# Reading the moving columns of single-pass matmuls as two interleaved halves

## The chip, the cores and the metric

The kernel runs on one core of one Trainium2 chip. The metric is the device time of one execution in microseconds, median of several runs. Three runs of the kernel before took 2629.4, 2629.59 and 2632.5 us; the median is 2629.59 us.

## The reference

Two layers follow each other. The first mixes along the sequence in the frequency domain: a real FFT over 3008 positions of each of 8 sequences of 256 features, a complex product with a 256x256 weight plus bias, a soft threshold of 0.01 on the real and the imaginary part, and the inverse FFT. The second is a feed-forward layer on the 24064 resulting tokens: 256 features to 2048, then `h*cos(h)`, then back to 256. Everything is float32.

```
X = np.fft.rfft(x, axis=1)                       # x: 8 x 3008 x 256
Yr = Xr @ w_r - Xi @ w_i + b_r                   # soft threshold on Yr, Yi follows
Yi = Xr @ w_i + Xi @ w_r + b_i
y = np.fft.irfft(Y, n=3008, axis=1)
h = y.reshape(24064, 256) @ moe_w_in             # to 2048
out = (h * np.cos(h)) @ moe_w_out                # back to 256
```

## The kernel before

3008 is 47 times 64, so the transform is done as a DFT of length 47, one of length 64, the mixing, an inverse DFT of length 64 and an inverse DFT of length 47. Each batch (one sequence) passes four stages.

- **Stage A** (`stage_a`, first DFT-47): 32 units of 512 columns. The input is split into a high and a low part; one matmul with the constant `fas` (line 364) gives both products on two sets of partitions, and ACT and DVE add them on the way out (lines 366 and 367) into `ao`, which goes to DRAM scratch. Batches 0 and 1 have forms of their own (`stage_a0`, `stage_a1`).
- **Stage B** (`stage_b`): 12 units. `fwd` is the DFT-64 (line 396). `wmix` mixes features with three sums of two weights, 18 matmuls of 256 columns (lines 420 to 422), then bias and threshold. `idft` is the inverse DFT-64, three matmuls of 512 columns (line 460; in unit 0 six of 256), copied out by ACT (line 463). Batch 0 has `stage_b0`.
- **Stage C** (`stage_c`, inverse DFT-47): line 715, results split into `xTh` and `xTl`, the tokens of the feed-forward layer.
- **Feed-forward** (`moe_step`, `second`): for each batch six tiles of tokens, five of 512 and one of 448, and for each tile 16 chunks of 128 of the 2048 features. A step of one tile and chunk has six matmuls into `ph` (lines 772 to 774) and, three steps later, six into `po` (lines 742, 743, 748). Between them ACT and DVE form `h*cos(h)` and split it into `gh` and `gl` (lines 779 to 785).

Precision comes from splitting: a number is written as a high and a low part of type float32r, and a product is three float32r matmuls (high by high, low by high, high by low). Four places use whole float32 operands instead: lines 396 and 715, and the transforms of batches 0 and 1. The profile names both types f32 in a matmul's row; a float32 matmul stands in it as two records, a float32r matmul as one.

The order is the program's own (`tc.manual_schedule`): each feed-forward step calls `pull`, which takes pieces of the next batches' stages A, B and C by a budget of costs (`share`, the numbers that the stages yield). So stage work of later batches stands between the feed-forward matmuls of this one. PSUM has three banks for `ph`, three for all stage work (`fps`), and two for `po`.

Every moving operand of a matmul is read in before with its columns one after another. The feed-forward output has one column per token, and the host puts tokens in order at the end.

Of the kernel before, what the change touches and what calls it, by code (L numbers as in the profile page):

```python
# [17 lines left out]
ALU = mybir.AluOpType  # L18

NB, N, D, FF = 8, 3008, 256, 2048  # L20
# [7 lines left out]
NTT = 6  # L28
# [29 lines left out]
def _index():  # L58
    n1, n2 = np.arange(64), np.arange(48)
    return (47 * n1[:, None] + 64 * n2[None, :]) % N  # L60


def _constants():
# [50 lines left out]
def tile_body(ctx: ExitStack, tc, x, x2, w_r, w_i, b_r, b_i, w_in, w_out,  # L114
              c_fa, c_fas, c_fb, c_inv, c_sig, c_last, c_inf, out):
    nc = tc.nc
# [12 lines left out]
    fas = cp.tile([112, 128], F32R, name="fas")  # L129
    ident = cp.tile([128, 128], F32, name="ident")  # L130
    inv = cp.tile([128, 2, 2, 128], F32R, name="inv")
# [8 lines left out]
    inf, ws = {}, []  # L140
    wf = cp.tile([128, 3, 2, 2, 256], F32R, name="wf")
    win = cp.tile([128, 2, 2, FF], F32R, name="win")
    wo = [cp.tile([128, 2, NFC, 256], F32R, name="wout")]

    mm = nc.tensor.matmul

    def rest_pool(lo, x, hi):
        return nc.gpsimd.tensor_tensor(out=lo, in0=x, in1=hi.bitcast(F32), op=ALU.subtract)  # L148

# [11 lines left out]
        nc.vector.scalar_tensor_tensor(out=wi, in0=wi, scalar=-1.0, in1=wr, op0=ALU.mult, op1=ALU.subtract)  # L161

    def split_fourier_w(j):
        hi, lo = (wf[:, j, h].rearrange("p c e -> p (c e)") for h in range(2))
        nc.scalar.copy(hi, ws[j])
        rest_pool(lo, ws[j], hi)

    def load_f64(src, queue):
        if len(raws) < EARLY_W + TAIL_W:
# [63 lines left out]
    raws, mark = [], {}  # L233
# [101 lines left out]
    def stage_a(b):  # L335

        scr1[b] = dr.tile([24, 2, 64, 256], F32, tag="scr1", name=f"scr1_{b}")
        dst = scr1[b].rearrange("k r n d -> (k r) (n d)")
        ld = {}

        def load(i):
            if i < 32:
                g, c = i % 2, i // 2
                ld[i] = stage_in("xt")[:112]
                nc.sync.dma_start(ld[i], x2[b - 2, g, :, 512 * c:512 * (c + 1)])

        def prep(i):
            if i < 32:
                xt = ld[i]
                ld[i] = wk.tile([128, 512], F32R, tag="xh", name="xh", bufs=XH_BUFS)[:112]  # L350
                with tc.issue_after(mark["gh"].ins) if b == 2 else ExitStack():
                    nc.scalar.copy(ld[i], xt)  # L352
                (rest if i % A_DVE == 0 else rest_pool)(ld[i][64:], xt[64:], ld[i][64:])

        load(0)
        yield 0.0
        prep(0)
        yield 1.0
        for i in range(32):
            load(i + 1)  # L360
            prep(i + 1)
            g, c = i % 2, i // 2
            p = fps("pa")
            mm(p, fas, ld.pop(i), start=True, stop=True)  # L364
            ao = stage_out("ao")[:48]
            nc.scalar.copy(ao, p[:48])  # L366
            nc.vector.tensor_tensor(out=ao, in0=p[64:112], in1=ao, op=ALU.add)  # L367
            nc.sync.dma_start(dst[:, 8192 * g + 512 * c:8192 * g + 512 * (c + 1)], ao)
            yield 0.23

    def stage_b(b):
        scr2[b] = dr.tile([32, 2, 2, 24, 256], F32, tag="scr2", name=f"scr2_{b}")
        dst = scr2[b].rearrange("j g r k d -> (j g r) (k d)")
        at, fb, X, Z, V = {}, {}, {}, {}, {}
# [40 lines left out]
        def wmix(m):  # L415
            xh, xl = X.pop(m)

            def product(p, j, comp, first, stop):
                for c in range(2):
                    mm(p, xh[:, comp, c], wf[:, j, 0, c], start=first and c == 0, stop=False, skip_group_check=True)  # L420
                    mm(p, xh[:, comp, c], wf[:, j, 1, c], start=False, stop=False, skip_group_check=True)  # L421
                    mm(p, xl[:, comp, c], wf[:, j, 0, c], start=False, stop=stop and c == 1, skip_group_check=True)  # L422

            p1 = fps("p1")[:, :256]
            product(p1, 0, 2, True, True)
            k1 = [wk.tile([128, 256], F32, tag=f"k1{r}", name=f"k1{r}", bufs=2) for r in range(2)]
            nc.vector.tensor_tensor(out=k1[1], in0=p1, in1=bias[:, 1], op=ALU.add)
            nc.vector.tensor_tensor(out=k1[0], in0=p1, in1=bias[:, 0], op=ALU.add)
            nc.scalar.activation(k1[1], k1[1], AF.Copy, scale=sig[:, m:m + 1])
            yield 0.73  # L430
            p2 = fps("p2")
            product(p2[:, :256], 1, 1, True, False)
            yield 0.73
            product(p2[:, 256:], 2, 0, False, True)
            z = wk.tile([128, 2, 256], F32, tag="z", name="z", bufs=2)
            for k in range(2):
                ks = slice(64 * k, 64 * k + 64)
                nc.vector.tensor_tensor(out=z[:64, k], in0=p2[ks, :256], in1=k1[0][ks], op=ALU.add)
            for k in range(2):
                ks = slice(64 * k, 64 * k + 64)  # L440
                nc.vector.scalar_tensor_tensor(out=z[64:, k], in0=p2[ks, 256:], scalar=sig[ks, m:m + 1],
                                               in1=k1[1][ks], op0=ALU.mult, op1=ALU.add)
            z = z.rearrange("p k e -> p (k e)")
            cl = wk.tile([128, 512], F32, tag="cl", name="cl", bufs=1)
            nc.vector.tensor_scalar(out=cl, in0=z, scalar1=-LAM, scalar2=LAM, op0=ALU.max, op1=ALU.min)  # L445
            nc.gpsimd.tensor_tensor(out=z, in0=z, in1=cl, op=ALU.subtract)  # L446
            yh = wk.tile([128, 512], F32R, tag="yh", name="yh", bufs=2)
            yl = wk.tile([128, 512], F32R, tag="yl", name="yl", bufs=2)
            nc.scalar.copy(yh, z)
            rest_pool(yl, z, yh)  # L450
            V[m] = (yh, yl)
            yield 0.73

        def idft(m):
            p = fps("pi")
            parts = ((0, 256, 0), (256, 512, 1)) if m == 0 else ((0, 512, 1),)
            y = V.pop(m)
            for n, (h, y) in enumerate(((0, y[0]), (1, y[0]), (0, y[1]))):
                for lo, hi, v in parts:
                    mm(p[:, lo:hi], inv[:, h, v], y[:, lo:hi], start=n == 0 and lo == 0, stop=n == 2 and hi == 512,  # L460
                       skip_group_check=True)
            bo = stage_out("bo")
            nc.scalar.copy(bo, p)
            nc.sync.dma_start(dst[:, 512 * m:512 * m + 512], bo)
            yield 0.68

# [266 lines left out]
    def second(b, t, f, gh, gl):  # L733
        n = 512 if t < NTT - 1 else 448
        first, last_f = next((lo, hi - 1) for v, lo, hi in phases(b) if v == t and lo <= f < hi)
        if f == first:
            outs[0] = [ps.tile([128, 512], F32, tag=f"o{e}", name=f"po{e}", bufs=1) for e in range(2)]
        po = outs[0]
        end = (b, t, f) == (NB - 1, NTT - 1, NFC - 1)
        for e in range(2):  # L740
            es = slice(128 * e, 128 * e + 128)
            mm(po[e][:, :n], wo[0][:, 0, f, es], gh[:, :n], start=f == first, stop=False)  # L742
            mm(po[e][:, :n], wo[0][:, 1, f, es], gh[:, :n], start=False, stop=False)  # L743
            if end:
                mm(po[e][:, :n], wo[0][:, 0, f, es], gl[:, :n], start=False, stop=True)
        for e in range(0 if end else 2):
            es = slice(128 * e, 128 * e + 128)
            mm(po[e][:, :n], wo[0][:, 0, f, es], gl[:, :n], start=False, stop=f == last_f)  # L748
        if f != last_f:
            return  # L750
        for e in range(2):
            if last_f < NFC - 1:
                part[t, e] = wk.tile([128, 512], F32, tag=("yh", "yl", "z")[t], name="part", bufs=2)
                nc.scalar.copy(part[t, e], po[e])  # L754
                continue
            if e == 0:
                outs[1] = pool["mo"].tile([128, 2, 512], F32, tag="ob", name="ob", bufs=1)
            ob = outs[1][:, e]
            if first:
                nc.vector.tensor_tensor(out=ob, in0=po[e], in1=part.pop((t, e)), op=ALU.add)  # L760
            else:
                (nc.vector.tensor_copy if end and e else nc.scalar.copy)(ob[:, :n], po[e][:, :n])
            nc.sync.dma_start(out[b, e, :, 512 * t:512 * t + n], ob[:, :n])

    def moe_step(b, t, f, pull):
        th, tl = xT[b, t]
        n = 512 if t < NTT - 1 else 448
        ph = ps.tile([128, 512], F32, tag="h", name="ph", bufs=3)
        h = ph[:, :n]
        fs = slice(128 * f, 128 * f + 128)  # L770
        for c in range(2):
            mm(h, win[:, 0, c, fs], th[:, c, :n], start=c == 0, stop=False)  # L772
            mm(h, win[:, 0, c, fs], tl[:, c, :n], start=False, stop=False)  # L773
            mark["ph"] = mm(h, win[:, 1, c, fs], th[:, c, :n], start=False, stop=c == 1)  # L774
        u = pool["mo"].tile([128, 512], F32, tag="u", name="u", bufs=4)
        k = u.bitcast(I32)
        gh = pool["mo"].tile([128, 512], F32R, tag="gh", name="gh", bufs=SKEW + 1)
# [143 lines left out]
```

## Time and profile before

| | |
|---|---|
| runs | 2629.4, 2629.59, 2632.5 us |
| the profiled execution | 2629.45 us |
| its span, first to last instruction | 2627.7 us |
| busy | PE 2618.9, PEld 2241.8, DVE 1917.8, ACT 1877.2, POOL 1085.3 us |
| granted TensorE clock | 1.00 over the span |
| instructions on PE | 13180 matmuls, 13180 weight loads |

The profiled execution is 0.14 us under the median of the runs. PE is the array's matmuls, PEld its weight loads. The duration of one matmul in a row is from its start to its last result and holds a fixed time in the pipeline that overlaps the next matmul; what one costs the engine is the distance from its start to the next one's start. That distance is called the pitch below.

### The profile page before, as it was taken

The page shows a single profiled execution, that of the slowest core. Times are in us where ns is not written, and L with a number is a line of the kernel's source. Part 1 is how long each engine was busy: PE and PEld are TensorE (multiplying, and loading weights), DVE is VectorE, ACT ScalarE, POOL GpSimd, SP SyncE. Part 2 cuts the span into 40 slices and gives each one's busy share as a digit, 9 for nine tenths or more (in the row PEclk, how much of TensorE's full clock was granted, in tenths as well). Part 3 has the DMA queues.
Part 4 walks back from the last instruction along what each step waited for, and adds up shares of the span by engine and source line. Part 5 has one row for each costly group of instructions (what it writes and reads, how often), then busy time and mean ns, then how long its engine had stood idle before and what let it go on. Part 6 is the DMA issues. An engine that isn't in the chain of part 4 may idle for free.

```text
span 2627.7 us, 38433 instructions
## 1 busy us (share of the span) xinstructions
PE 2618.9 (100%) x13180; PEld 2241.8 (85%) x13180; DVE 1917.8 (73%) x3237; ACT 1877.2 (71%) x3557; POOL 1085.3 (41%) x916
## 2 busy tenths in 40 slices
PE   9999999999999999999999999999999999999999
PEld 8788888888888888888888888888888888888888
DVE  6888876877667776777767777677776666766665
ACT  5787766777677776777767777677776666666666
POOL 5774543544334443344423444244442333322222
PEclk9999999999999999999999999999999999999999
DMA  7533312322123222233212232123221111010000
GB/s 208 177 97 98 105 61 77 94 87 90 55 60 93 86 85 59 60 93 98 75 56 62 91 96 75 55 62 103 89 71 53 47 53 43 25 54 22 9 17 16
DMA packets 126373, 194.26 MB, mean 74 GB/s; under 512 B 14131, under 2 KB 63619, under 8 KB 126177
## 3 DMA queue, kind: packets, MB, share of 16 engines
q1 hardware_dynamic: 120160, 171.94, 21.5%
q0 software_dynamic: 6016, 19.86, 2.4%
q8 instruction: 104, 1.70, 0.3%
q14 instruction: 93, 0.75, 0.1%
HBM read 119.92 MB, written 71.83 MB: 73 GB/s over the span
## 4 chain that ended last, share of the span: by engine, by line
PE 99%; DMA 0%; DVE 0%; SPq 0%; issue 0%; ACT 0%; ACTq 0%
PE ph L772 13%; PE po L742 13%; PE po L743 13%; PE ph L773 13%; PE po L748 13%; PE ph L774 13%; PE pc L715 4%; PE pb L396 3%; PE p L422 2%; PE p L421 2%; PE p L420 2%; PE pi L460 2%; PE pa L364 2%; PE p L520 1%; PE pa L323 1%; PE pa L297 0%
## 5 line engine op out<-in xcount | busy, mean ns | idle before, releaser
L148 POOL TENSOR_TENSOR gl<-u,gh 128x512 fp32r<-128x512 f32 (+1 forms) x396 | 507.8, 1283 | 958.0 <-ACT gh L784 754.9
L783 DVE TENSOR_TENSOR u<-ph,u 128x512 f32<-128x512 f32 (+1 forms) x768 | 520.5, 678 | 275.6 <-ACT u L782 258.5
L780 DVE SCALAR_TENSOR_TENSOR u<-ph,u 128x512 f32<-128x512 f32 (+1 forms) x768 | 518.9, 676 | 252.0 <-ACT u L779 242.4
L779 ACT ACTIVATE u<-ph 128x512 int32<-128x512 f32 (+1 forms) x768 | 450.1, 587 | 253.0 <-PE ph L774 241.2
L782 ACT ACTIVATE u<-u 128x512 f32<-128x512 f32 (+1 forms) x768 | 479.5, 625 | 202.1 <-DVE u L780 199.1
L772 PE MATMUL ph<-xTh,win 128*128 128x512 f32 (+1 forms) x1536 | 611.5, 398 | 1.4 <-DVE u L783 1.1
L742 PE MATMUL po<-gh,wout 128*128 128x512 f32 (+1 forms) x1536 | 598.7, 390 | 0.0
L774 PE MATMUL ph<-xTh,win 128*128 128x512 f32 (+1 forms) x1536 | 595.1, 387 | 0.0
L773 PE MATMUL ph<-xTl,win 128*128 128x512 f32 (+1 forms) x1536 | 595.1, 387 | 0.0
L743 PE MATMUL po<-gh,wout 128*128 128x512 f32 (+1 forms) x1536 | 594.8, 387 | 0.0
L784 ACT CAST gh<-u 128x512 fp32r<-128x512 f32 (+1 forms) x768 | 467.2, 609 | 137.1 <-DVE u L783 134.9
L748 PE MATMUL po<-gl,wout 128*128 128x512 f32 (+1 forms) x1534 | 477.0, 388 | 0.0
L774 PEld LDWEIGHTS ph<-xTh,win 128*128 128x128 f32 x1536 | 288.8, 188 | 54.4
L742 PEld LDWEIGHTS po<-gh,wout 128*128 128x128 f32 x1536 | 289.0, 188 | 51.7 <-ACT part L754 0.3
L743 PEld LDWEIGHTS po<-gh,wout 128*128 128x128 f32 x1536 | 289.0, 188 | 51.6
L772 PEld LDWEIGHTS ph<-xTh,win 128*128 128x128 f32 x1536 | 289.1, 188 | 49.6 <-DVE u L783 2.0
L748 PEld LDWEIGHTS po<-gl,wout 128*128 128x128 f32 x1534 | 285.6, 188 | 51.9
L773 PEld LDWEIGHTS ph<-xTl,win 128*128 128x128 f32 x1536 | 289.5, 188 | 46.0
L151 DVE TENSOR_TENSOR gl<-u,gh 128x512 fp32r<-128x512 f32 (+1 forms) x372 | 274.2, 737 | 49.8 <-ACT gh L784 42.2
L148 POOL TENSOR_TENSOR xh<-xt,xh 48x512 fp32r<-48x512 f32 x144 | 188.5, 1310 | 205.9 <-ACT xh L352 179.4
L446 POOL TENSOR_TENSOR z<-z,cl 128x512 f32<-128x512 f32 x84 | 110.0, 1309 | 208.4 <-DVE cl L445 197.6
L367 DVE TENSOR_TENSOR ao<-pa,ao 48x512 f32<-48x512 f32 x192 | 133.0, 693 | 22.2 <-ACT ao L366 17.1
(122 smaller groups left out, 3108.1 us busy)
## 6 DMA issues: line engine op xcount, KB each, us to landing
xt<-in_dram SPq DMA_DIRECT2D x192, 224.0 KB, 2.7
scr<-bo SPq DMA_DIRECT2D x95, 256.0 KB, 2.0
bt<-scr SPq DMA_DIRECT2D x96, 240.0 KB, 3.2
at<-scr SPq DMA_DIRECT2D x84, 256.0 KB, 2.7
out_dram<-ob SPq DMA_DIRECT2D x80, 256.0 KB, 2.2
scr<-ao SPq DMA_DIRECT2D x192, 96.0 KB, 1.9
fb<-in_dram POOLq DMA_DIRECT2D x46, 256.0 KB, 3.3
raw<-in_dram POOLq DMA_DIRECT2D x14, 512.0 KB, 4.3
```

The lines of the kernel that those rows point to most:

```text
L148: return nc.gpsimd.tensor_tensor(out=lo, in0=x, in1=hi.bitcast(F32), op=ALU.subtract)
L742: mm(po[e][:, :n], wo[0][:, 0, f, es], gh[:, :n], start=f == first, stop=False)
L743: mm(po[e][:, :n], wo[0][:, 1, f, es], gh[:, :n], start=False, stop=False)
L748: mm(po[e][:, :n], wo[0][:, 0, f, es], gl[:, :n], start=False, stop=f == last_f)
L772: mm(h, win[:, 0, c, fs], th[:, c, :n], start=c == 0, stop=False)
L773: mm(h, win[:, 0, c, fs], tl[:, c, :n], start=False, stop=False)
L774: mark["ph"] = mm(h, win[:, 1, c, fs], th[:, c, :n], start=False, stop=c == 1)
L779: nc.scalar.activation(k[:, :n], h, AF.Identity, bias=0.25, scale=1.0 / TWO_PI)
L780: nc.vector.scalar_tensor_tensor(out=u[:, :n], in0=h, scalar=1.0 / TWO_PI, in1=k[:, :n], op0=ALU.mult, op1=ALU.subtract)
L782: nc.scalar.activation(u[:, :n], u[:, :n], AF.Sin, bias=HALF_PI, scale=TWO_PI)
L783: nc.vector.tensor_tensor(out=u[:, :n], in0=h, in1=u[:, :n], op=ALU.mult)
L784: mark["gh"] = nc.scalar.copy(gh[:, :n], u[:, :n])
```

## The change

Three views are added: `woven` reads a row of n columns in the order 0, n/2, 1, n/2+1, and so on; `unwoven` and `halves` are used by evictions to bring such a row back in order. `woven` is put on the moving operand of the float32r matmuls of the feed-forward layer (both products), of the mixing, of the inverse DFT-64 in units 1 to 11, and of stage A. The columns come out of the array in the woven order:

- In the feed-forward layer nothing undoes it: `ph` is woven once, `po` twice, all vector work between is column by column, and the host's index takes the double permutation (`_order`).
- In the mixing the weight is the moving operand. Its split form `wf` is stored in the opposite order once, so that the woven read gives the natural one.
- In the inverse DFT-64 and in stage A the evictions read PSUM with a step of two columns and write two contiguous halves.

```
+    def woven(v):
+        return v.rearrange("p (b a) -> p a b", b=2)
+    def unwoven(v):
+        return v.rearrange("p (a b) -> p b a", b=2)
+    def halves(v):
+        return v.rearrange("p (b a) -> p b a", b=2)
     def split_fourier_w(j):
-        hi, lo = (wf[:, j, h].rearrange("p c e -> p (c e)") for h in range(2))
-        nc.scalar.copy(hi, ws[j])
-        rest_pool(lo, ws[j], hi)
+        for c in range(2):
+            hi, lo = (woven(wf[:, j, h, c]) for h in range(2))
+            w = ws[j][:, 256 * c:256 * c + 256].rearrange("p (a b) -> p a b", b=2)
+            nc.scalar.copy(hi, w)
+            rest_pool(lo, w, hi)
...
-            mm(p, fas, ld.pop(i), start=True, stop=True)
+            mm(p, fas, woven(ld.pop(i)), start=True, stop=True)
             ao = stage_out("ao")[:48]
-            nc.scalar.copy(ao, p[:48])
-            nc.vector.tensor_tensor(out=ao, in0=p[64:112], in1=ao, op=ALU.add)
+            nc.scalar.copy(halves(ao), unwoven(p[:48]))
+            nc.vector.tensor_tensor(out=halves(ao), in0=unwoven(p[64:112]), in1=halves(ao), op=ALU.add)
...
-                    mm(p, xh[:, comp, c], wf[:, j, 0, c], start=first and c == 0, stop=False, skip_group_check=True)
+                    wh, wl = (woven(wf[:, j, h, c]) for h in range(2))
+                    mm(p, xh[:, comp, c], wh, start=first and c == 0, stop=False, skip_group_check=True)
...
-                    mm(p[:, lo:hi], inv[:, h, v], y[:, lo:hi], start=n == 0 and lo == 0, stop=n == 2 and hi == 512,
+                    mm(p[:, lo:hi], inv[:, h, v], woven(y) if m else y[:, lo:hi], start=n == 0 and lo == 0,
...
+            if m:
+                nc.scalar.copy(halves(bo), unwoven(p))
+            else:
+                nc.scalar.copy(bo, p)
...
-            mm(po[e][:, :n], wo[0][:, 0, f, es], gh[:, :n], start=f == first, stop=False)
+            mm(po[e][:, :n], wo[0][:, 0, f, es], woven(gh[:, :n]), start=f == first, stop=False)
...
-            mm(h, win[:, 0, c, fs], th[:, c, :n], start=c == 0, stop=False)
+            mm(h, win[:, 0, c, fs], woven(th[:, c, :n]), start=c == 0, stop=False)
```

The lines of the other matmuls of these products change in the same way. No instruction changes its place on any engine. The only rows that differ are the six that split the mixing weights `wr`, `wi` and `wc` into `wf` in the prologue. On ACT these stood before as

```order
L515 COPY Xf<-pb 128x512
L165 CAST wf<-wr 128x512
L326 COPY ao<-pa 96x512
L515 COPY Xf<-pb 128x512
L165 CAST wf<-wi 128x512
L326 COPY ao<-pa 96x512
L165 CAST wf<-wc 128x512
L201 ACTIVATE wm<-raw 128x512
```

and on ACT they stand now, with the line numbers of the changed kernel, as

```order
L539 COPY Xf<-pb 128x512
L185 CAST wf<-wr 128x128x2 x2
L346 COPY ao<-pa 96x512
L539 COPY Xf<-pb 128x512
L185 CAST wf<-wi 128x128x2 x2
L346 COPY ao<-pa 96x512
L185 CAST wf<-wc 128x128x2 x2
L221 ACTIVATE wm<-raw 128x512
```

Each of the three became two of half the size at the same place; the three subtractions on POOL that follow them did too.

## Rows read from the trace of the kernel before

**Rows 1.** The page, part 1: busy us (share of the span) xinstructions.

```profile
span 2627.7 us, 38433 instructions
...
PE 2618.9 (100%) x13180; PEld 2241.8 (85%) x13180; DVE 1917.8 (73%) x3237; ACT 1877.2 (71%) x3557; POOL 1085.3 (41%) x916
```

**Rows 2.** The page, part 4: the chain that ended last, by engine.

```profile
PE 99%; DMA 0%; DVE 0%; SPq 0%; issue 0%; ACT 0%; ACTq 0%
```

**Rows 3.** Timeline of PE: start us, us, engine line op out<-in xcount; feed-forward of 512.

```profile
2442.25 0.39 PE L772 MATMUL ph<-xTh,win 128*128 128x512 f32 x1
...
2450.41 0.39 PE L772 MATMUL ph<-xTh,win 128*128 128x512 f32 x1
```

**Rows 4.** Timeline of PE, feed-forward of 448 columns, up to the end.

```profile
2612.35 0.36 PE L772 MATMUL ph<-xTh,win 128*128 128x448 f32 x1
...
2617.21 0.36 PE L772 MATMUL ph<-xTh,win 128*128 128x448 f32 x1
...
2622.89 0.57 PE L745 MATMUL po<-gl,wout 128*128 128x448 f32 x2
```

**Rows 5.** Timeline of PE, mixing products of 256 columns.

```profile
1222.14 0.28 PE L420 MATMUL p<-wf,Xh 128*128 128x256 f32 x1
...
1222.85 0.40 PE L772 MATMUL ph<-xTh,win 128*128 128x512 f32 x1
1223.08 0.28 PE L420 MATMUL p<-wf,Xh 128*128 128x256 f32 x1
...
1224.16 0.40 PE L364 MATMUL pa<-xh,fas 112*128 112x512 f32 x1
```

**Rows 6.** Timeline of PE, float32 matmuls of 256 and 512 columns in the prologue.

```profile
76.10 1.03 PE L520 MATMUL p<-wr,Xf 128*128 128x256 f32 x4
...
78.69 1.02 PE L528 MATMUL pi<-z,inf 128*128 128x512 f32 x2
...
87.58 3.60 PE L323 MATMUL pa<-xq,fa 96*96 96x512 f32 x8
91.01 1.88 PE L323 MATMUL pa<-xt,fa 96*96 96x512 f32 x4
```

**Rows 7.** Timeline of all engines: a matmul and the next weight load.

```profile
2442.48 0.39 PE L773 MATMUL ph<-xTl,win 128*128 128x512 f32 x1
2442.49 0.19 PEld L774 LDWEIGHTS ph<-xTh,win 128*128 128x128 f32 x1
```

**Rows 8.** Line 520: xcount: duration ns min/median/max, first and last start us, forms.

```profile
L520 PEld LDWEIGHTS p<-wr,Xf x48: 187/190/192, 25.6 to 80.8; 128*128 128x128 f32 x48
```

**Rows 9.** Windows: us, busy us (xcount) of each engine, PEclk, DMA share, GB/s.

```profile
2617.00:2622.90 5.90, 5.90 (x31) 5.46 (x30) 3.49 (x6) 2.98 (x6) 1.16 (x1) 1.00 0.00 0
```

**Rows 10.** Groups by line and shape on PE: xcount | busy us, mean ns | idle.

```profile
L773 PE MATMUL ph<-xTl,win 128*128 128x512 f32 x1280 | 501.1, 391 | 0.0
...
L420 PE MATMUL p<-wf,Xh 128*128 128x256 f32 x504 | 142.5, 283 | 0.0
...
L773 PE MATMUL ph<-xTl,win 128*128 128x448 f32 x256 | 94.0, 367 | 0.0
...
L460 PE MATMUL pi<-yh,inv 128*128 128x512 f32 x154 | 47.5, 390 | 0.0
```

**Rows 11.** Timeline of PE, a stretch with other stage work near.

```profile
1204.71 0.40 PE L772 MATMUL ph<-xTh,win 128*128 128x512 f32 x1
...
1205.64 0.39 PE L773 MATMUL ph<-xTl,win 128*128 128x512 f32 x1
```

**Rows 12.** Groups by line and shape on ACT and DVE.

```profile
L367 DVE TENSOR_TENSOR ao<-pa,ao 48x512 f32<-48x512 f32 x192 | 133.0, 693 | 22.2 <-ACT ao L366 17.1
...
L299 ACT COPY a<-pa 128x384 f32<-128x384 f32 x8 | 3.9, 490 | 13.8 <-PE pa L297 13.8
...
L724 ACT CAST xTh<-pc 128x386 fp32r<-128x386 f32 x8 | 3.8, 470 | 0.3 <-DVE xTl L725 0.3
```

More of the change, by code (lines that the diff above doesn't have):

```diff
@@ L60, in _index, with _order @@
     return (47 * n1[:, None] + 64 * n2[None, :]) % N
+def _order():
+    at = []
+    for t in range(NTT):
+        n = min(512, N - 512 * t)
+        w = np.arange(n).reshape(2, n // 2).T.reshape(-1)
+        at.append(512 * t + w[w])
+    return np.concatenate(at)
 def _constants():
@@ L419, in product @@
                 for c in range(2):
-                    mm(p, xh[:, comp, c], wf[:, j, 0, c], start=first and c == 0, stop=False, skip_group_check=True)
-                    mm(p, xh[:, comp, c], wf[:, j, 1, c], start=False, stop=False, skip_group_check=True)
-                    mm(p, xl[:, comp, c], wf[:, j, 0, c], start=False, stop=stop and c == 1, skip_group_check=True)
+                    wh, wl = (woven(wf[:, j, h, c]) for h in range(2))
+                    mm(p, xh[:, comp, c], wh, start=first and c == 0, stop=False, skip_group_check=True)
+                    mm(p, xh[:, comp, c], wl, start=False, stop=False, skip_group_check=True)
+                    mm(p, xl[:, comp, c], wh, start=False, stop=stop and c == 1, skip_group_check=True)
             p1 = fps("p1")[:, :256]
@@ L459, in idft @@
                 for lo, hi, v in parts:
-                    mm(p[:, lo:hi], inv[:, h, v], y[:, lo:hi], start=n == 0 and lo == 0, stop=n == 2 and hi == 512,
-                       skip_group_check=True)
+                    mm(p[:, lo:hi], inv[:, h, v], woven(y) if m else y[:, lo:hi], start=n == 0 and lo == 0,
+                       stop=n == 2 and hi == 512, skip_group_check=True)
             bo = stage_out("bo")
-            nc.scalar.copy(bo, p)
+            if m:
+                nc.scalar.copy(halves(bo), unwoven(p))
+            else:
+                nc.scalar.copy(bo, p)
             nc.sync.dma_start(dst[:, 512 * m:512 * m + 512], bo)
@@ L741, in second @@
             es = slice(128 * e, 128 * e + 128)
-            mm(po[e][:, :n], wo[0][:, 0, f, es], gh[:, :n], start=f == first, stop=False)
-            mm(po[e][:, :n], wo[0][:, 1, f, es], gh[:, :n], start=False, stop=False)
+            mm(po[e][:, :n], wo[0][:, 0, f, es], woven(gh[:, :n]), start=f == first, stop=False)
+            mm(po[e][:, :n], wo[0][:, 1, f, es], woven(gh[:, :n]), start=False, stop=False)
             if end:
-                mm(po[e][:, :n], wo[0][:, 0, f, es], gl[:, :n], start=False, stop=True)
+                mm(po[e][:, :n], wo[0][:, 0, f, es], woven(gl[:, :n]), start=False, stop=True)
         for e in range(0 if end else 2):
             es = slice(128 * e, 128 * e + 128)
-            mm(po[e][:, :n], wo[0][:, 0, f, es], gl[:, :n], start=False, stop=f == last_f)
+            mm(po[e][:, :n], wo[0][:, 0, f, es], woven(gl[:, :n]), start=False, stop=f == last_f)
         if f != last_f:
@@ L771, in moe_step @@
         for c in range(2):
-            mm(h, win[:, 0, c, fs], th[:, c, :n], start=c == 0, stop=False)
-            mm(h, win[:, 0, c, fs], tl[:, c, :n], start=False, stop=False)
-            mark["ph"] = mm(h, win[:, 1, c, fs], th[:, c, :n], start=False, stop=c == 1)
+            mm(h, win[:, 0, c, fs], woven(th[:, c, :n]), start=c == 0, stop=False)
+            mm(h, win[:, 0, c, fs], woven(tl[:, c, :n]), start=False, stop=False)
+            mark["ph"] = mm(h, win[:, 1, c, fs], woven(th[:, c, :n]), start=False, stop=c == 1)
         u = pool["mo"].tile([128, 512], F32, tag="u", name="u", bufs=4)
@@ L918 @@
     res = np.empty((NB, N, D), np.float32)
-    res[:, idx[:, :47].reshape(2, 32, 47).transpose(1, 0, 2).reshape(-1)] = got
+    res[:, idx[:, :47].reshape(2, 32, 47).transpose(1, 0, 2).reshape(-1)[_order()]] = got
     return res.reshape(NB * N, D)
```

## The prediction

> **What bounds the kernel now.** I read the page's busy times first, then the chain that ended last, then the timeline of PE in stretches of one kind of matmul. PE is busy for the whole span of 2627.7 us, DVE for 73% and ACT for 71% of it [rows 1], and the chain is PE for 99% [rows 2]. So the time is the sum of the matmuls' pitches, and the question is what a matmul's pitch is made of.
>
> Feed-forward steps of 512 columns: from 2442.25 to 2450.41 there are three steps, 36 matmuls, in 8.16 us: 226.7 ns each [rows 3]. With 448 columns: 24 matmuls in 4.86 us, 202.5 ns [rows 4]. Mixing products of 256: six in 0.71 and nine in 1.08 us, 119.3 ns [rows 5]. From 256 to 512 columns the pitch grows by 107.4 ns, 0.42 ns a column, one tick at the level of 2.4 GHz, which the granted clock of 1.00 [rows 9] means. One column a tick makes 213.3, 186.7 and 106.7 ns; what is left over is 13.4, 15.8 and 12.6 ns per matmul, nearly the same at every width.
>
> The float32 matmuls of the prologue have no such rest. Twelve records of 256 columns take 2.59 us, 215.8 ns each, and eight of 512 take 3.43 us, 428.8 ns [rows 6]. Here the growth is 0.83 ns a column, so a record spends two ticks on a column, and 2.1 to 2.5 ns are left over. Both kinds have the next weight load beside them: it starts 0.01 us after the matmul before it has started and lasts 0.19 us [rows 7], and 190 ns in the float32 case [rows 8]. So the weight load itself isn't the rest. What differs is that float32r wants a new column at every tick.
>
> The rest isn't the other engines' doing either. In the last 5.9 us DVE is busy 3.49, ACT 2.98 and POOL 1.16 us and no DMA moves [rows 9], and the pitch there is that of before: 28 matmuls from 2617.21 to 2622.89, 202.9 ns [rows 4].
>
> **The change part by part.** No instruction moves, none is added to PE, and no wait is added anywhere. Each float32r matmul now takes its columns from two places half a row apart, in turn. The array's work (one tick a column) is untouched; only the rest can shrink, or the supply of columns can fall below one a tick. No matmul of before reads its moving columns out of order, so both sides are bounded by the nearest rows.
>
> *Lower end.* The rest falls to that of the float32 records, 2.5 ns, so the pitches become 215.8, 189.2 and 109.2 ns:
> - feed-forward of 512: six lines of 1280 [rows 10], 7680 times 10.9 ns, 83.7 us;
> - feed-forward of 448: six lines of 256, 1536 times 13.3 ns, 20.4 us;
> - mixing: three lines of 504, 1512 times 10.1 ns, 15.3 us;
> - inverse DFT-64: 154 and half as many of its third matmul, 231 [rows 10], times 10.9 ns, 2.5 us;
> - stage A: 192 units (as many as `ao` additions [rows 12]) times 10.9 ns, 2.1 us.
>
> Together 124.0 us. There are also stretches, between stage work, where 512 columns take longer: four matmuls in 0.93 us, 232.5 ns [rows 11]. The mean duration of line 773 is 391 ns over the trace [rows 10] against 389 in clean rows, so this adds some 2 ns a matmul, 8103 times, 16 us, to what could go: 140 us in all.
>
> *Upper end.* If a place can't give a column at every second tick out of order, the supply drops to the float32 records' two ticks a column: 428.8 for 226.7 ns (8103 times 202.1 ns, 1637.6 us), 375.8 for 202.5 ns (1536 times 173.3, 266.2 us) and 215.8 for 119.3 ns (1512 times 96.5, 145.9 us): plus 2050 us.
>
> Between the two I take the lower end without the slow stretches, minus 124 us. The reason: what the rows tie the rest to is a supply at full rate from one place while the weight load reads beside it. In the new order each of the two places gives a column every second tick, which is what one place gives in the float32 rows, where the rest is 2.5 ns. That is the nearest row to the new pattern, if alternating between places is free in itself. I leave the slow stretches where they are, since some follow a switch between float32 and float32r that stays.
>
> *Evictions.* `ao` and `bo` are read from PSUM with a step of two. Line 299 already reads PSUM with a step and takes 490 ns for 384 elements on ACT; line 724 takes 470 for 386 in order [rows 12]. That is 4%, 28 ns on an `ao` addition of 693 ns. ACT and DVE have over a quarter of the span free [rows 1], and PE goes on with feed-forward matmuls in other banks meanwhile: nothing. If PE had to wait for all of it: 192 times 28 ns, 5 us; if each addition took double, 133 us.
>
> *Mixing weights.* Three more instructions on ACT and three on POOL in the prologue, where PE works on float32 matmuls for batch 0; `wf` is not read before batch 1's mixing. Nothing; uncovered, about 0.2 us each.
>
> *What is late next.* A feed-forward step of twelve matmuls falls from 2.72 to 2.59 us. DVE's share rises to 1917.8/2503.7, 77%, and ACT's to 75%; neither becomes the bound, though single waits may appear on PE.
>
> The sum: 2629.45 minus 124.0 is 2505.5 us for an execution like the profiled one, which is 0.14 us under the median. I predict 2505 us. Of this kernel a difference of 0.2%, 5.3 us, is about what a measurement can tell from no change.
>
> **The rivals.**
>
> *Only the slow stretches go.* If the even rest belongs to starting any float32r matmul, only what comes on top of it (rows 11 against rows 3) depends on how columns are read: minus 16 us, 2613 us. For it: the rest is the same at 256 and at 512 columns, like a cost of starting. Against: 448 columns have a larger rest than 512.
>
> *It doesn't do what it says.* The rest is of the float32r form and the reading order plays no part: 2629 us. The quiet end with its unchanged pitch speaks for it, since nothing else was there to collide with. Against it stands only that the same loads and starts cost 2.5 ns in float32. [...]
>
> *Slower: alternating places costs a tick.* The supply may count on neighbours: a fetch that brings several adjacent columns serves the next ticks too, and a jump at every column throws that away. The place is every float32r matmul. It decides from 10.9 ns per 512 columns on, one lost tick in twenty columns. At one lost tick in every column it is the upper end, 2629 plus 2050, 4679 us; at one in four, a quarter of it, some 3140 us. For it: 0.42 ns a column in rows 3 and 5 is the array's own rate, so the supply in order is at least that fast and nothing shows a reserve for a worse order. Against: each place is still read in order, so the neighbours come up two ticks later, and a fetch that is kept for two places loses nothing. [...]
>
> *Evictions hold PE.* The doubled `ao` addition above, 133 us, on the unchanged pitch: 2762 us; in part, some 2650.
>
> **How the numbers follow.** The full gain, between 2470 (the 140 us, and most of the 28 us that 2.5 ns on 11151 matmuls make, if no rest at all stays) and 2580 us (a part of the rest stays): 0.52. Only the slow stretches, about 2613: 0.13. No change: 0.10. Slower by lost ticks: 0.19. Slower by evictions: 0.06. Hence faster 0.65, same 0.10, slower 0.25. The likeliest case alone reaches from 2470 to 2580. The range goes on to 2660, over the next two and the small losses, and leaves out the lost ticks, which begin anywhere and end at 4679.
>
> **What would show it.** Right: a run of 36 feed-forward matmuls in about 7.77 us in place of 8.16, six products in 0.66 us, the float32 rows unchanged, PE still over 98% of the chain. Wrong: a pitch of 226 ns as before (then the order plays no part), of 300 ns or more (then neighbours matter), or gaps on PE before lines 364 and 460 (then the evictions do). If the pitch falls as said but the time doesn't, PE's waits must show who took it.

## The result and the profile after

The changed kernel takes 2503.44 us (median of 4 runs, 2502.70 to 2504.38), the kernel before beside it on the same chip 2629.49 us. The ratio is 0.9518, with a 95% interval from 0.9502 to 0.9535: 126 us less. The profiled execution took 2503.21 us.

The page of the changed kernel, busy times (as in [rows 1]) and the chain by engine (as in [rows 2]):

```profile
span 2501.4 us, 38461 instructions
...
PE 2486.2 (99%) x13180; PEld 2241.9 (90%) x13180; DVE 1912.0 (76%) x3237; ACT 1856.1 (74%) x3560; POOL 1075.8 (43%) x919
...
PE 81%; DVE 8%; ACT 6%; issue 3%; DMA 1%; POOL 0%; ACTq 0%; POOLq 0%; DVEq 0%; SPq 0%
```

PE does the same 13180 matmuls and weight loads in 133 us less. The other engines have the work of before, and PE now stands still here and there: 1% of the span, which is enough for the chain to go over DVE and ACT where it did not before. A chain leaves PE at each wait, however short, and may then stay on the other engines for a while; its 81% doesn't say that PE is free for 19%.

The timeline of PE, feed-forward of 512 columns, to be set beside [rows 3]. The line numbers of the feed-forward layer are higher by 24 than before:

```profile
2317.63 0.38 PE L796 MATMUL ph<-xTh,win 128*128 128x512 f32 x1
...
2325.40 0.38 PE L796 MATMUL ph<-xTh,win 128*128 128x512 f32 x1
...
2489.03 0.35 PE L796 MATMUL ph<-xTh,win 128*128 128x448 f32 x1
...
2493.57 0.35 PE L766 MATMUL po<-gh,wout 128*128 128x448 f32 x1
```

From 2317.63 to 2325.40 there are 36 matmuls in 7.77 us, 215.8 ns each, where it was 226.7. The last two lines are the 448 columns, beside [rows 4]: 24 matmuls in 4.54 us, 189.2 ns, where it was 202.5. From 448 to 512 columns it is 26.6 ns, 0.416 ns a column, 2.4 columns a ns: the tick that the prediction counts with. What is left over one tick a column (213.3 and 186.7 ns), the rest in the prediction's word, is 2.5 ns at either width.

Mixing products of 256 columns, same view, beside [rows 5]:

```profile
1171.84 0.27 PE L441 MATMUL p<-wf,Xh 128*128 128x256 f32 x1
...
1172.73 0.28 PE L443 MATMUL p<-wf,Xl 128*128 128x256 f32 x1
1172.84 0.38 PE L384 MATMUL pa<-xh,fas 112*128 112x512 f32 x1
```

Nine products start in 1.00 us, 111.1 ns each, where it was 119.3. That is 4.4 ns over a tick a column, not 2.5. The float32 records stay as they were: twelve of 256 columns in 2.59 us, as in [rows 6]:

```profile
75.78 1.03 PE L544 MATMUL p<-wr,Xf 128*128 128x256 f32 x4
...
78.37 1.02 PE L552 MATMUL pi<-z,inf 128*128 128x512 f32 x2
```

Groups by line and shape, the mixing on PE (beside [rows 10]), then the evictions (beside [rows 12]) and the mixing weights:

```profile
L441 PE MATMUL p<-wf,Xh 128*128 128x256 f32 x504 | 139.4, 277 | 2.1 <-ACT bo L485 0.9 <-DVE xTl L749 0.8 <-DVE ao L387 0.2
...
L387 DVE TENSOR_TENSOR ao<-pa,ao 48x512 f32<-48x512 f32 x192 | 133.0, 693 | 15.0 <-ACT ao L386 8.9 <-DMA xt<-in_dram 0.6
...
L386 ACT COPY ao<-pa 48x512 f32<-48x512 f32 x192 | 109.7, 571 | 0.9 <-PE pa L384 0.4
...
L485 ACT COPY bo<-pi 128x512 f32<-128x512 f32 x77 | 44.4, 576 | 8.1 <-PE pi L481 8.0
...
L185 ACT CAST wf<-wr 128x256 fp32r<-128x256 f32 x2 | 1.1, 667 | 0.0
```

The `ao` addition, which now reads PSUM with a step of two, takes 693 ns as before. Line 441 (420 before) had no idle time before it and now has 2.1 us in all. The waits of PE, the largest of the list; columns are what waited, for what, us in total, times, longest:

```profile
PE ph L796 <- DVE u L807: 1.8, 3, 0.9
PE pa L384 <- DVE Xl L430: 1.7, 6, 0.4
...
PE po L766 <- ACT part L778: 1.2, 1, 1.2
PE pc L739 <- DMA bt<-scr: 1.0, 1, 1.0
```

PE's gaps of over 100 ns add up to 11.05 us in 21 places, before to 4.5 us in 7 (both worked out from the trace). One of them, in the timeline of all engines:

```profile
150.72 0.60 ACT L803 ACTIVATE u<-ph 128x512 int32<-128x512 f32 x1
151.21 1.08 ACT L778 COPY part<-po 128x512 f32<-128x512 f32 x2
...
151.85 0.48 PE L766 MATMUL po<-gh,wout 128*128 128x512 f32 x1 [1.19 <-ACT part L778]
```

The first `po` matmul of a tile needs ACT to have copied the last tile's `po`. ACT does that in its turn, after the activation of `u`, and PE, faster by 5% in a step, is there first. Eleven of the 21 gaps lie between 100 and 400 us, where PE is busy for 294.17 of 300 us; from 1000 to 1300 it is for 299.71:

```profile
100.00:400.00 300.00, 294.17 (x1563) 262.66 (x1562) 256.71 (x428) 237.83 (x461) 175.43 (x149) 1.00 0.33 98
1000.00:1300.00 300.00, 299.71 (x1606) 271.92 (x1605) 235.81 (x401) 230.36 (x448) 131.97 (x112) 1.00 0.27 82
```

The account, each kind's sum of start-to-start distances, worked out from both traces: feed-forward of 512 from 1779.4 to 1684.0 us (minus 95.4); of 448 from 318.2 to 295.3 (minus 22.9); mixing from 180.7 to 172.9 (minus 7.8); inverse DFT-64 from 52.5 to 49.8 (minus 2.7); stage A from 46.0 to 47.1 (plus 1.1, waits included: its median pitch fell from 233 to 220 ns). Together minus 127.7; the float32 matmuls, not changed, take 1.4 more with their waits, and the spans differ by 126.3.

### The profile page after: what moved, and what is told of

It is laid out like the page before. It is cut to its first block, busy times and chain, and to the rows that moved or that the text cites. A ratio compares the mean times of both kernels' runs of the same rounds, so it can differ in the third digit from the quotient of the medians.

```text
span 2501.4 us, 38461 instructions
## 1 busy us (share of the span) xinstructions
PE 2486.2 (99%) x13180; PEld 2241.9 (90%) x13180; DVE 1912.0 (76%) x3237; ACT 1856.1 (74%) x3560; POOL 1075.8 (43%) x919
## 4 chain that ended last, share of the span: by engine, by line
PE 81%; DVE 8%; ACT 6%; issue 3%; DMA 1%; POOL 0%; ACTq 0%; POOLq 0%; DVEq 0%; SPq 0%
PE po L766 11%; PE po L772 11%; PE po L767 11%; PE ph L796 11%; PE ph L798 11%; PE ph L797 11%; PE pc L739 3%; PE pb L416 2%; DVE u L807 2%; PE pi L481 2%; PE p L442 2%; PE p L443 2%; PE p L441 2%; ACT u L806 2%; DVE u L804 1%
## 5 line engine op out<-in xcount | busy, mean ns | idle before, releaser
L166 POOL TENSOR_TENSOR gl<-u,gh 128x512 fp32r<-128x512 f32 (+1 forms) x396 | 501.8, 1268 | 874.6 <-ACT gh L808 447.7
L796 PE MATMUL ph<-xTh,win 128*128 128x512 f32 (+1 forms) x1536 | 592.3, 386 | 2.1 <-DVE u L807 1.8
L766 PE MATMUL po<-gh,wout 128*128 128x512 f32 (+1 forms) x1536 | 579.9, 378 | 1.3 <-ACT part L778 1.2
L798 PE MATMUL ph<-xTh,win 128*128 128x512 f32 (+1 forms) x1536 | 576.6, 375 | 0.0
L767 PE MATMUL po<-gh,wout 128*128 128x512 f32 (+1 forms) x1536 | 575.9, 375 | 0.0
L797 PE MATMUL ph<-xTl,win 128*128 128x512 f32 (+1 forms) x1536 | 575.6, 375 | 0.0
L772 PE MATMUL po<-gl,wout 128*128 128x512 f32 (+1 forms) x1534 | 458.1, 376 | 0.0
```

Source lines behind the costliest of these rows:

```text
L766: mm(po[e][:, :n], wo[0][:, 0, f, es], woven(gh[:, :n]), start=f == first, stop=False)
L767: mm(po[e][:, :n], wo[0][:, 1, f, es], woven(gh[:, :n]), start=False, stop=False)
L772: mm(po[e][:, :n], wo[0][:, 0, f, es], woven(gl[:, :n]), start=False, stop=f == last_f)
L796: mm(h, win[:, 0, c, fs], woven(th[:, c, :n]), start=c == 0, stop=False)
L797: mm(h, win[:, 0, c, fs], woven(tl[:, c, :n]), start=False, stop=False)
L798: mark["ph"] = mm(h, win[:, 1, c, fs], woven(th[:, c, :n]), start=False, stop=c == 1)
```

## The experiments

The prediction had the size but only a guess at the cause. The expectations number several theories. Before the first run: **theory 1**, collision, the prediction's reason: a stream at one column a tick from one place meets the reads of the weight load beside it. **Theory 2**, the jump: it helps when a column doesn't lie near the one before. **Theory 3**, the form: the rest is a cost of float32r that any two-dimensional order avoids.

After that run the author had two more theories. By both the distance between the two places plays no part; by the second any two places in turn are free, wherever they start. What the memory does with a row of columns no run looks at: what stands below are pitches by order. In the third run **theory C**: the order as such, two alternating places help float32r and any two-dimensional order slows float32.

**Orders behind the kernel's last matmul.** 21 stretches of 32 matmuls each, one order each. X(k) is a row of 512 columns of `win`, W(k) 128 columns of `wout`, and the stretches differ in the view of one of them. They add work whose result nothing reads.

```
+    for k in range(32):  # halves
+        with tc.issue_after(prev.ins): prev = mm(pt[k % 2], W(k), X(k).rearrange("p (b a) -> p a b", b=2), start=True, stop=True)
```

> The changed kernel with 21 runs of 32 more float32r matmuls behind its last one (their results go to PSUM and are not used; the output is the reference's). Moving operand: rows of w_in in SBUF; stationary: w_out. Each run has another reading order or another number of stationary columns. Theory 1, collision: a stream at one column a tick from one place meets the reads of the weight load beside it; two places at half the rate don't. Then in order 227 ns, halves, quarters and eighths 216, steps of 2, 4 or 8 columns (one place at a time) not better than 227; with 64 and 32 stationary columns in order the rest of 13 ns falls to about 8 and 5, since the load is shorter. Theory 2, the jump: what helps is that each column comes from another line of memory than the one before. Then steps of 4 and 8 give 216 too, while chunks of 4 or 8 columns from each half in turn stay near 227. Theory 3, the form: the rest is a cost of starting a float32r matmul with one-dimensional columns. Then every two-dimensional pattern gives 216 and 64 or 32 stationary columns still give 227.

Timeline of PE in that run. A row is one stretch of 32 (start, us); the pitch is the distance to the next stretch's start divided by 32 (or, where the next isn't shown, the row's length less 0.16 us, by which neighbours overlap, divided by 32):

```profile
2498.09 7.45 PE L927 MATMUL pt<-win,wout 128*128 128x512 f32 x32
2505.39 7.07 PE L929 MATMUL pt<-win,wout 128*128 128x512 f32 x32
2512.29 9.21 PE L931 MATMUL pt<-win,wout 128*128 128x512 f32 x32
2521.34 15.77 PE L933 MATMUL pt<-win,wout 128*128 128x512 f32 x32
2536.91 14.64 PE L935 MATMUL pt<-win,wout 128*128 128x512 f32 x32
...
2598.61 7.95 PE L945 MATMUL pt<-win,wout 128*128 128x512 f32 x32
...
2613.30 7.07 PE L949 MATMUL pt<-win,wout 128*128 128x512 f32 x32
2620.21 7.43 PE L951 MATMUL pt<-win,wout 128*128 128x512 f32 x32
...
2634.85 7.58 PE L955 MATMUL pt<-win,wout 128*32 128x512 f32 x32
```

In order 228 ns (L927), halves 216 (L929), quarters 283 (L931), eighths 487 (L933), every second column first 452 (L935). In rows not shown: pairs from each half in turn 333, chunks of 4 from each half 250, steps of 4 and 8 461 and 431. Chunks of 8 from each half take 243 (L945). Alternating single columns of two neighbouring blocks of 4 gives 216 (L949), of two neighbouring blocks of 2 gives 227 (L951). So two places far apart aren't needed: blocks of 4 columns next to each other do the same. Theory 2 wanted 216 for steps of 4 and 8, theory 3 for every two-dimensional order, theory 1 for quarters and eighths; none of this came. And 256 columns take 120 in order and 112 in halves, as in the kernel.

The weight load was shortened at L955 (32 stationary columns in place of 128), the loads' own rows from the two stretches:

```profile
L927 PEld LDWEIGHTS pt<-win,wout x32: 187/188/189, 2497.9 to 2504.9; 128*128 128x128 f32 x32
...
L955 PEld LDWEIGHTS pt<-win,wout x32: 107/108/112, 2634.6 to 2641.8; 128*32 128x32 f32 x32
```

The load falls from 188 to 108 ns, and the pitch in order doesn't fall with it, it is 232 (64 columns: 134 ns, 230). Theory 1 wanted a smaller rest there, so it falls by this too. In rows not shown, one weight and one row repeated 32 times take 227 as well, and a weight read in steps of two takes 233 with the columns in order and 216 in halves.

**Where blocks begin, and how long they are.** The same way, with other orders, alignments and float32 operands:

> The changed kernel with 18 runs of 32 more matmuls behind its last one, as in the first run of this kind; the output is the reference's. Known from that run: in order 227 to 228 ns, two halves 215.8, blocks of 16 or 4 columns exchanged with their neighbour block 215.8, blocks of 2 columns 227, four quarters 283, eighths 487, steps of 2, 4 or 8 columns 431 to 461. The number of stationary columns played no part, so the weight load is out. [...] 128 columns in order 67 by a fixed rest of 13 (not seen if the weight load takes 109 to 112). [...]

```profile
2513.82 7.45 PE L931 MATMUL pt<-win,wout 128*128 128x504 f32 x32
...
2534.81 8.69 PE L937 MATMUL pt<-win,wout 128*128 128x504 f32 x32
2543.33 6.97 PE L939 MATMUL pt<-win,wout 128*128 128x504 f32 x32
...
2558.72 3.69 PE L943 MATMUL pt<-win,wout 128*128 128x128 f32 x32
2562.24 3.73 PE L945 MATMUL pt<-win,wout 128*128 128x128 f32 x32
2565.81 7.83 PE L947 MATMUL pt<-win,wout 128*128 128x512 f32 x32
2573.48 7.10 PE L949 MATMUL pt<-win,wout 128*128 128x512 f32 x32
2580.42 7.42 PE L951 MATMUL pt<-win,wout 128*128 128x512 f32 x32
2587.68 13.97 PE L953 MATMUL pt<-win,wout 128*128 128x256 f32 x64
2601.49 17.65 PE L955 MATMUL pt<-win,wout 128*128 128x256 f32 x64
2618.97 28.32 PE L957 MATMUL pt<-win,wout 128*128 128x256 f32 x64
```

- Blocks of 4 with the row started two columns later: 227 (L951), where they took 216 (L949 of the run before). So it matters where the blocks start in the row, and the theory by which any two places in turn are free, which wanted 216 here, falls. Halves one column off stay at 217 (L949), in order one column off takes 240 (L947).
- Blocks of 3 take 266 (L937) and blocks of 6 take 213 for 504 columns, 2.8 ns over a tick a column (L939). The author had expected 216 to 235 for both: a miss on either side. The 504 columns in order take 228 (L931), no less than 512.
- 128 columns take 110 in order and 112 in halves (L943, L945): half the columns of the mixing's 256 and the same pitch. So in these stretches the pitch stops falling near 110 ns. The mixing's 111 to 112 is close to that; that the same holds it there is not shown.
- float32 in order takes 216 a record (L953), in halves 273 (L955), in quarters 440 (L957). The author had expected 216 for halves and quarters, and at most 230 for a step of 4, which took 451 (not shown): three misses.

**Each column twice.** A float32 record in order spends two ticks on a column (215.8 ns for 256) and has a rest of 2.5 ns; float32r spends one and has 13.4. Whether two ticks on a column make the difference can be tried on float32r by reading each of 256 columns twice:

> The changed kernel with 9 runs of 32 more matmuls behind its last one; the output is the reference's. Known so far: for float32r, blocks of 4 exchanged 215.8 ns, the same blocks started 2 columns off 226.9, in order 227 to 228, quarters 283; for float32 with 256 columns, in order 215.8 a record, halves 273, quarters 440, a step of 4 columns 451. [...] Theory C, order as such: float32 is slowed by any two-dimensional order, and float32r helped by any with two alternating places. Then reading each column twice gives 227, and float32 gives 273 for exchanged blocks of 2 and chunks of 4 too.

```profile
2496.37 7.45 PE L927 MATMUL pt<-win,wout 128*128 128x512 f32 x32
2503.66 7.07 PE L929 MATMUL pt<-win,wout 128*128 128x512 f32 x32
2510.56 13.98 PE L931 MATMUL pt<-win,wout 128*128 128x256 f32 x64
2524.38 17.65 PE L933 MATMUL pt<-win,wout 128*128 128x256 f32 x64
2541.86 17.66 PE L935 MATMUL pt<-win,wout 128*128 128x256 f32 x64
2559.35 13.98 PE L937 MATMUL pt<-win,wout 128*128 128x256 f32 x64
2573.17 13.98 PE L939 MATMUL pt<-win,wout 128*128 128x256 f32 x64
2586.98 14.67 PE L941 MATMUL pt<-win,wout 128*128 128x256 f32 x64
```

float32r with each column twice, still in order: 216 (L929) against 228 (L927). Theory C had 227 here, and 273 for float32 in every two-dimensional order; it falls. The float32 rows (64 records each): in order 216 (L931); halves 273 and blocks of 4 in turn 273 (L933, L935); blocks of 2 in turn 216 (L937); chunks of 4 from each half 216 (L939); chunks of 2 from each half 227 (L941, where the last record starts just ahead of the float32r row that follows, so that 14.3 us are 63 pitches). So some two-dimensional orders cost float32 nothing, and blocks of 4 in turn, which take float32r from 228 to 216, cost it as much as halves do.

**Parts of the change.** Only the feed-forward layer woven; and only mixing, inverse DFT-64 and stage A.

```
-            mm(p, fas, woven(ld.pop(i)), start=True, stop=True)
+            mm(p, fas, ld.pop(i), start=True, stop=True)
...
-                    mm(p[:, lo:hi], inv[:, h, v], woven(y) if m else y[:, lo:hi], start=n == 0 and lo == 0,
-                       stop=n == 2 and hi == 512, skip_group_check=True)
+                    mm(p[:, lo:hi], inv[:, h, v], y[:, lo:hi], start=n == 0 and lo == 0, stop=n == 2 and hi == 512,
+                       skip_group_check=True)
```

This is the first kernel, against the changed one; its mixing and evictions are those of before too. The second kernel has `woven` in these three stages and not in `moe_step` and `second`.

> Only the feed-forward matmuls read in two halves; mixing, inverse DFT-64 and stage A as before. If each matmul gains by itself (theory 1 to 3): feed-forward of 512 at 215.8 in place of 231.7 to 226.7 ns, 95 us over the trace, of 448 at 189.2, 23 us, less some 5 us of new waits on PE: 2629.5 - 113 = 2516 us. If the gain came from the evictions or the stages (rival): near 2629.

> Only mixing, inverse DFT-64 of units 1 to 11 and stage A read in two halves, with their evictions and the split of the mixing weights; feed-forward as before. If each matmul gains by itself: 1512 products from 119.5 to 111.6 ns, 12 us, 231 of the inverse at 11 ns, 2.5 us, 192 of stage A at 12 ns, 2.3 us, together 17 us: 2612 us. If the strided evictions hold PE: above 2620.

Measured: 2517.31 us (2515.75 to 2518.84), ratio 0.957 [0.9554, 0.9586], and 2617.54 us (2616.16 to 2620.14), 0.9953 [0.9938, 0.9967]; the kernel before ran at 2629.95 us beside them. Minus 112.6 and minus 12.4 make minus 125, nearly the whole of 126. The totals add up, though not kind by kind. In the trace of the second kernel the mixing alone gives 11.6 us, the inverse DFT-64 2.7 and stage A 2.7, the 17 us expected; what is missing is that the feed-forward matmuls of 512 columns, still in order, take 3.9 us more (1783.3 for 1779.4 us). In the changed kernel the mixing gives only 7.8. The second kernel's gain, 0.5%, is small, but clear of 1 by its interval.

**Neighbouring blocks of 4 in the whole kernel.** The views alternate between neighbouring blocks of 4 columns in place of halves:

```
-        return v.rearrange("p (b a) -> p a b", b=2)
+        return v.rearrange("p (g b a) -> p g a b", b=2, a=4)
```

> As the changed kernel, but in place of the two halves of a row, blocks of 4 columns are exchanged with their neighbour block of 4: order 0, 4, 1, 5, 2, 6, 3, 7, 8, 12, and so on; evictions, weight split and the host's index follow. By both theories of the matmul run the distance doesn't matter: pitches 215.8, 189.2 and 111.6 ns as with halves, 2503 us, the same within 0.2%. If only far places help in the whole kernel (rival): 2600 or more.

Measured: 2501.94 us (2500.11 to 2503.29), ratio 0.9511 [0.9495, 0.9527]. The same gain with the two places 4 columns apart: the distance plays no part in the kernel either.

**Quarters in the feed-forward layer.** The same view with `b=4`, nothing else woven:

> Feed-forward only, and its rows are read in four quarters in turn instead of two halves; everything else as before the change. From the run of orders 283 ns for 512 columns in place of 227 and 216: 7680 times 67 ns, and 1536 times 59 ns (448 columns in proportion) more than the feed-forward-only kernel's 2517: 3120 us. If the real kernel hides part of it or the order only counts for repeated weights: less. If any interleaving helped as such: 2517.

Measured: 3077.06 us, ratio 1.1698 [1.1674, 1.1721]. A piece of its timeline, PE:

```profile
2323.49 0.45 PE L754 MATMUL po<-gh,wout 128*128 128x512 f32 x1
2323.77 0.45 PE L755 MATMUL po<-gh,wout 128*128 128x512 f32 x1
```

280 ns where halves take 216. A loss as in the rival that the prediction called lost ticks does come; it begins one step further, with four places. The kernel came 43 us under the 3120 expected: by the traces, 27 at 512 columns (2170.1 us in all, against 1683.0 in the feed-forward-only kernel, 63 ns a matmul where 67 were expected) and 16 at 448 (median 238 ns).

**Can the new waits be had back?** With blocks of 4, unit 0 of the inverse DFT-64 can be woven too, and `FIRST_A`, which sets how much stage A work stands early in batch 0, was moved from `(0, 0, 0.5, 0)` to `(0, 0, 0.25, 0.25)` in one kernel and to `(0, 0, 0, 0.25)` in another:

```
-FIRST_A = (0.0, 0.0, 0.5, 0.0)
+FIRST_A = (0.0, 0.0, 0.0, 0.25)
```

> Exchanged blocks of 4 columns as in the near run, now in unit 0 of the inverse DFT-64 too (42 matmuls of 256 columns, 8 ns each, 0.3 us), and the stage A work of batch 2 that stood in the third phase of batch 0 is spread over the third and the fourth (a quarter each). In the near run 9.4 us of PE's time are waits, some 5 us of them between 100 and 350 us. If these come from too much stage work in the third phase: 2498 us. If the waits move on to the fourth phase: 2502 us as before, within 0.2%.

> The same with no stage A work in the third phase and a quarter of it in the fourth, so more is left for the phases after that. If the third phase alone was too full: 2498 us. If the later phases, which get more, wait instead: 2503 us or more.

Measured: 2500.51 us (2500.32 to 2503.21), 0.9511 [0.9495, 0.9527], and 2499.29 us (2498.64 to 2499.44), 0.9502 [0.9488, 0.9517]; the first lies between its two forecasts. Their gaps on PE are 9.2 and 9.0 us, against 9.4 with blocks of 4 alone, so moving the work took away little. To see whether the gain is there at all, the changed kernel and the second of these ran beside each other on one chip:

> The changed kernel once more, beside the next kernel on the same chip: 2503 us, as before, within 0.1%.

> The kernel with exchanged blocks of 4 and stage A's early work moved to the fourth phase, once more. If its 4 us against the changed kernel are its own (fewer waits on PE): 2499 us here, 4 us under the changed kernel on this chip, with no overlap of their runs. If they came from another chip: both the same within 1 us.

Measured: 2503.16 us (2502.61 to 2504.11), 0.9519 [0.9506, 0.9532], and 2499.61 us (2498.83 to 2502.01), 0.9508 [0.9495, 0.9521]. The runs don't overlap, as was forecast, and the medians differ by 3.5 us, 0.14%. The two ratios' intervals overlap, and 0.14% is less than the 0.2% that the prediction said can be told apart: probably a better version, but the step is too small to be called shown, and which of its three edits makes it stays open.

## Why the prediction was right, and where it was not

**The time.** 2505 was predicted, 2503.4 came. The term that carried the sum, a rest that falls to 2.5 ns, was right at 512 and 448 columns, to 0.1 ns. The closeness of the total owes something to two misses that cancel:

- *Slow stretches left standing.* The prediction kept 16 us for them. They went too: the feed-forward terms, 83.7 and 20.4 us, measured 95.4 and 22.9, 14.2 us more. The traces say where. In the kernel before, 2881 of the 7680 distances of 512 columns are 228 to 242 ns; behind a mixing or a stage A matmul the first averages 234 to 237, and it takes ten to twelve to come back to 226.7. In the changed kernel, and in the one with only the feed-forward layer woven, nearly all are 214 to 221 ns but for some 240 of about 300 ns, directly behind a float32 matmul; with only the stages woven, 3061 are slow. So the slow stretches belong to reading in order ([rows 11], 232.5 ns) and not to the switch, which stayed. What makes the rest in order larger there was not tried; a row started one or two columns further, 240 and 233 ns, shows that it isn't one number even without neighbours.
- *Mixing and waits.* 15.3 us were forecast for the mixing and 7.8 came. 119.3 minus 111.6 ns (the mean of line 442) is 7.7 and not 10.1 ns a product: 11.6 us, which the stages-only kernel shows. Of the 3.8 us still missing, 2.8 are seven distances from a last mixing product to a stage A matmul, six of which hold the waits `pa L384 <- DVE Xl L430`. That the pitch stops falling near 110 ns (128 columns) was in no row before. Stage A's 2.1 us became plus 1.1 with its waits. "Single waits may appear on PE" was the one cost named without a size; the gaps grew by 6.5 us.

**The reason given.** It was wrong, and the sum came out in spite of it. "A supply at full rate from one place while the weight load reads beside it" has two halves, and both fell: a weight load 80 ns shorter leaves the pitch at 232 ns, and reading from one place (neighbouring blocks of 4, or each column twice in order) takes 216 too. Half the rate is not what helped the float32 rows: float32 in halves, at the same half rate, lost 57 ns a record. The comparison with [rows 6] gave the right size for a wrong reason, and that was luck: why float32 in order has a rest of only 2.5 ns no run shows. For quarters the same argument (each place at a quarter of the rate) would have forecast a gain too, and that kernel takes 3077 us.

**The rivals.** *Lost ticks* came for four places (283 ns at 512 columns, 3077 us for the kernel) and not for two (216 ns). Its argument, a fetch that brings neighbours and can be kept for two places, was the author's guess; no run looks at a fetch. What the runs show is the pitch of each order: 216 ns for halves, the least here at 512 columns; 216 for neighbouring blocks of 4 and 227 with those started two columns off; 452 for every second column first. *It doesn't do what it says* (no change) fell with each column read twice, 216 ns against 228. *Evictions* with a step take no longer: 693, 571 and 576 ns, where it was 693, 575 and 581. The 4% that the prediction took from lines 299 and 724 is 5% by the element; neither came.

**What would show it.** 7.77 us for 36 matmuls and unchanged float32 rows came as written. Six products in 0.66 us came as 0.67. Of the signs of being wrong, gaps before line 364 (now 384), seven did appear, 2.3 us; by the trace DVE's `Xl` and `xh` ended them and not an eviction of `ao`. "PE over 98% of the chain" did not come: the chain is PE for 81% with PE busy for 99%. The chain's share was the wrong sign to name; busy time and the list of waits are the right ones.

**Correction.** Ahead of the prediction the text says that `tc.manual_schedule` orders the whole program. It orders the prologue; in the main part a scheduler places what the pulls issue. The order on each engine is still that of before, so no step hangs on it.

**Open.** Why reading in order leaves about the same over the ticks at 512 and at 256 columns (13.4 and 12.6 ns) and not a share of each column, and why 504 columns take as long as 512. Why chunks of 4 and 8 columns from each half take 250 and 243 ns. Why eighths take 487 ns where quarters take 283 and six places 291, and why four neighbouring blocks of 4 in turn take 268. Why blocks of 3 take 266 and blocks of 6 have 2.8 ns of rest. What makes one order faster than another at all: the runs show pitches, and none shows their cause.

## What to carry to other kernels

When matmuls stand back to back, compare the pitch with a tick per column at the granted clock (0.416 ns at 1.00 here); a few per cent above it, with no wait in the trace, is worth a trial of the reading order. For float32r columns, alternate between two halves of a row or two neighbouring blocks of 4 columns that start where they did here (216 ns for 228 at 512 columns; two columns off, 227), and put columns in order where it is free (a host index, a stored weight, an eviction). Don't go to four places (283 ns), and don't do it to float32 operands: 256 columns of those lose 27% by it (273 ns for 216).

## What was unexpected of the hardware

- Reading in order is not the fastest way to read float32r: 228 against 216 ns at 512 columns, in stretches behind everything else. Reading every column twice in order is faster than reading 512 columns once (216 against 228).
- The same interleaving that saves 5% on float32r costs float32 27% (216 to 273 ns a record).
- Float32r matmuls in a row, each with its own weight load, take 110 ns at 128 columns and hardly more, 112, at 256 in halves.
- A shorter weight load, 108 for 188 ns, changed the pitch from 228 to 232 ns, not downwards.
- Reads of PSUM with a step of two cost neither ACT nor DVE anything (571 to 693 ns as before); a write to SBUF that alternates between two halves did cost ACT time: 667 ns for 256 columns of `wf`, 1.1 us for the two that overlap, where 512 in order took 622 ns in the kernel before.
